# Strassen's algorithm for the last product of a fused three-block kernel, with squares made in the key stage and other buffers for the third-slot sums

## The chip, the core and the metric

The kernel runs on one core of a Trainium2 chip. The core has five engines with an instruction queue each: PE (TensorE, the matrix engine; PEld is its weight load), DVE (VectorE), ACT (ScalarE), POOL (GpSimd) and SP (SyncE, which here only starts DMAs). Matmuls write to PSUM, eight banks of 512 f32 columns on 128 partitions; all other tiles lie in SBUF. The metric is the device time of one execution in microseconds (us), as the median of several runs.

## What is computed

Three blocks follow one another, over 8 batches of 576 tokens (4608 tokens).

```python
# 1. attention by a feature map, 8 heads of 64, phi(x) has 256 features
proj = x @ w_phi; proj -= max|proj|; phi = [exp(proj), exp(-proj)]
kv = phi(k).T @ v; z = sum(phi(k)); attn = (phi(q) @ kv) / (phi(q) @ z)
# 2. four experts of causal softmax attention, head 64, top-2 gates
y_e = softmax(mask((x wq_e)(x wk_e).T / 8)) (x wv_e) wo_e;  x2 = sum_e gate_e * y_e
# 3. token shift and a gated square-ReLU block, 512 -> 1024 -> 512
xk = mu_k * x2 + (1 - mu_k) * x2_prev;  xr likewise with mu_r
k = max(xk @ w_k, 0);  v = (k * k) @ w_v;  r = sigmoid(xr @ w_r);  out = r * v
```

All products are of f32 accuracy: each operand is split into a rounded part (hi, type f32r) and the rest (lo), and three matmuls hi·hi, hi·lo and lo·hi are summed. The last product, (k * k) @ w_v, is 4608 x 1024 x 512. The inputs `w_k`, `w_v` and `w_r` come as 64-bit numbers and are decoded on the chip.

## The kernel before

Five streams of work are written out by Python generators and woven by `weave` (lines 54 to 74), which always takes the next step of the stream that is furthest behind in a virtual time of its own; the costs that steps return and the rates in lines 820 and 826 set that. A scheduler of the language then puts each engine's instructions in an order by these priorities and its own timeline. What a reader finds in the profile is that final order.

- `favors` (lines 250 to 394 and 640 to 663): block 1, batch by batch. Tiles `raw`, `hi`, `lo`, `pj`, `pm`, `ph`, `kv`, `num`, `xt`; the result goes to `XT`. When it is through, its memory is released and `pW` is opened: the last product's weights are loaded from DRAM tiles `wd` into `wst2` and split into `wvh2` and `wvl2` (page names `wvh`, `wvl`).
- `moe1` (lines 397 to 638): block 2. Tiles `qk`, `vp`, `sc` (scores), `a` (softmax), `at` (its transpose), `yp`, `yf`. Each batch's result `yt` is stored to DRAM as `yd`.
- `compose` and `decodes` (lines 188 to 230): the weights. `compose` multiplies the experts' output weights into the token-shifted `w_r` and `w_k` and stores twelve blocks `wf`; `decodes` decodes the sixteen pieces of `w_v` and stores them as `wd`.
- `gates_keys` (lines 676 to 746): the key stage. Tokens are taken in six chunks of 768, as 384 pairs of an even and an odd token. A chunk has twelve units u of 128 outputs (u 0 to 3 gates, u 4 to 11 keys), and each unit three slots `sl`: the product of slot 0 is common to both tokens, those of slots 1 and 2 are added to it for the even and the odd one. One product is six matmuls of 128x384 in a PSUM bank `rk` or `kv`, with weights `wt` loaded on ACT's queue, five buffers deep. ACT evacuates slot 0 into `z` (line 696), DVE adds slots 1 and 2 to it (line 698), and the sum is stored to DRAM tile `kd` on SP's queue (line 699). All `z` lie in one set of four buffers, tag `e`.
- `moe2` (lines 750 to 813): the last product, chunk by chunk and parity by parity. `kt_` loads two units of keys (`kx`), ACT takes ReLU and square in place (lines 777 and 778), DVE makes hi and lo in `XT` (lines 99 and 100), and PE multiplies with `wvh2` and `wvl2`, 96 matmuls of 128x384 into four PSUM banks `vacc` (line 792 through 117). DVE multiplies each bank by the gates `zs`, after ACT's sigmoid (line 764), into `o` (line 802), which is stored to the output.

`weave` in line 820 runs until `moe1` has ended. Then block 2's memory and PSUM banks are released (`phA.close()`), `psB` and `pB` are opened, and line 826 weaves what is left: the end of the key stage (its last chunk may not start earlier) with the last product. The text calls what follows `phA.close()` the last stage.

Of the kernel before, what the change touches and what calls it, by code (L numbers as in the profile page):

```python
# [76 lines left out]
def fused_kernel(ctx: ExitStack, tc: tile.TileContext, qT, kT, vx, wphi, wq, wk, wvg, wo, mu, w64, ident, cmask, tri, out):  # L77
# [9 lines left out]
    wd = [dram.tile([P, 256], F32, name=f'wd{i}') for i in range(NW)]  # L87
# [37 lines left out]
    pQ = ctx.enter_context(tc.tile_pool(name='pQ', bufs=1, side='right'))  # L125
# [514 lines left out]
    def favors():  # L640
# [16 lines left out]
        wv2.extend(pW.tile([P, 8, DM], F32R, name=n) for n in ('wvh2', 'wvl2'))  # L657
        for f in range(8):
            s_ = pW.tile([P, 768], F32, name='wst2', tag='wst2', bufs=2)[:, :512]
            for j in range(2):  # L660
                nc.sync.dma_start(s_[:, j * 256:(j + 1) * 256], wd[24 + 2 * f + j])
            split(wv2[0][:, f], wv2[1][:, f], s_, 'a', nc.gpsimd)
            yield 2000
    wv2 = []
# [11 lines left out]
    def gates_keys():  # L676

        def one(c):
# [3 lines left out]
            def unit(n):  # L682
# [9 lines left out]
                def ev():  # L692
                    z = pR.tile([P, HC], F32, name='z', tag='e', bufs=4)
# [56 lines left out]
    def moe2():  # L750

        def chunk(c, par, os):
            t0 = c * CH
            d = {}
            m = 2 * c + par

            def gate(g):

                def ld():
                    d['z', g] = late['pB'].tile([P, 2, HC], F32, name='zs', tag='zs', bufs=4)  # L760
                    nc.sync.dma_start(d['z', g], kd[c][:, 2 * g:2 * g + 2, par])

                def go():
                    nc.scalar.activation(d['z', g], d['z', g], AF.Sigmoid)
                return [(lambda: 'pB' in late, ld), None, go]

            def kt_(p):

                def ld():
                    if 4 * m + p < 2:  # L770
                        d['s', p] = late['pW'].tile([P, 2 * HC], F32, name='kx', tag='wst2', bufs=2).rearrange('p (u t) -> p u t', u=2)
                    else:
                        d['s', p] = late['pB'].tile([P, 2, HC], F32, name='kx', tag='kx', bufs=6)
# [100 lines left out]
```

## Time and profile before

| | |
|---|---|
| median of 3 runs | 1287.65 us (1284.47 to 1289.37) |
| profiled execution | 1288.14 us, span of its instructions 1286.3 us |
| PE busy | 1241.5 us, 97% of the span |
| DVE busy | 877.7 us, 68% |
| ACT busy | 733.0 us, 57% |
| POOL busy | 412.6 us, 32%, none of it after 1020 us |
| granted clock of TensorE | 0.995 of full speed on the mean |
| DMA | 208.78 MB, 162 GB/s on the mean |

PE has the longest bar and is seldom idle. Busy time of PE is a modelled one: matmuls overlap, and what one costs in a full stream is the distance of two starts, not its duration. So a stretch of the chain of waits in which PE alone stands, divided by the matmuls in it, gives the price of a matmul. Short shares of idle time lie at three places: before 400 us, between 800 and 1045 us, and at the very end, when the last results are stored.

### The profile page before, as it was taken

How to read it: one execution, taken by the hardware profiler on the slowest of the kernel's cores; microseconds unless marked ns; L12 is line 12 of the kernel's file. 1: busy time of each engine (PE TensorE's matmuls, PEld its weight loads, DVE VectorE, ACT ScalarE, POOL GpSimd, SP SyncE). 2: the span in 40 equal slices, each digit the busy share in tenths (PEclk: the TensorE clock that was granted, in tenths of full speed). 3: DMA queues.
4: the chain of work that ended last, by engine and by line, in shares of the span. 5: the costliest groups of instructions: out<-in, count | busy, mean ns of one | idle time of the engine just before them, and what ended most of it. 6: DMA issues, size and time to landing. Idle time of an engine off the chain costs nothing.

```text
span 1286.3 us, 26695 instructions
## 1 busy us (share of the span) xinstructions
PE 1241.5 (97%) x9152; PEld 1201.2 (93%) x9152; DVE 877.7 (68%) x2476; ACT 733.0 (57%) x1836; POOL 412.6 (32%) x570
## 2 busy tenths in 40 slices
PE   8999999999999999999999999879999989999998
PEld 7999989999999999999999999868988989999998
DVE  6766988788977877876788778546677464443441
ACT  5655767678767665665766565645445474333330
POOL 5532566455633323452444343322112100000000
PEclk9999999999999999999999999999999999999999
DMA  6323125322236444455344434766959887988741
GB/s 189 92 75 100 61 81 164 110 73 75 96 99 190 128 116 133 135 167 182 106 138 138 119 103 141 221 192 199 297 179 278 280 287 242 292 287 285 247 146 50
DMA packets 175127, 208.78 MB, mean 162 GB/s; under 512 B 20497, under 2 KB 160145, under 8 KB 174993
## 3 DMA queue, kind: packets, MB, share of 16 engines
q1 hardware_dynamic: 96656, 136.28, 32.6%
q10 hardware_dynamic: 78336, 70.80, 19.3%
q8 instruction: 74, 1.21, 0.4%
q14 instruction: 61, 0.49, 0.1%
HBM read 143.58 MB, written 63.44 MB: 161 GB/s over the span
## 4 chain that ended last, share of the span: by engine, by line
PE 80%; DVE 7%; DMA 5%; ACT 4%; POOL 2%; issue 1%; ACTq 0%; POOLq 0%; DVEq 0%; SPq 0%
PE rk L117 15%; PE vacc L117 14%; PE kv L327 10%; PE num L365 8%; PE qk L117 6%; PE vp L117 4%; PE yp L580 3%; PE at L545 3%; PE pj L275 3%; PE pj L276 2%; PE pj L277 2%; PE fo L117 2%; PE tq L349 2%; PE sc L507 2%; PE sc L508 2%
## 5 line engine op out<-in xcount | busy, mean ns | idle before, releaser
L117 PE MATMUL vacc<-XT,wvh 128*128 128x384 f32 x768 | 198.8, 336 | 3.9 <-DVE o L802 3.5
L100 POOL TENSOR_TENSOR lo<-raw,hi 128x256 fp32r<-128x256 f32 (+1 forms) x160 | 109.7, 688 | 213.7 <-ACT hi L97 203.3
L538 POOL TENSOR_SCALAR a<-a,sv,gw 128x128 f32<-128x128 f32 (+4 forms) x160 | 107.5, 674 | 213.9 <-DVE sv L532 76.1
L117 PEld LDWEIGHTS vacc<-XT,wvh 128*128 128x128 f32 x768 | 139.7, 189 | 4.6 <-DVE o L802 3.9
L365 PE MATMUL num<-kvs,ph 128*128 128x65 f32 (+1 forms) x1280 | 143.7, 262 | 0.0
L365 PEld LDWEIGHTS num<-kvs,ph 128*128 128x128 f32 (+1 forms) x1280 | 137.4, 181 | 4.9 <-issue 1.8
L117 PE MATMUL vacc<-XT,wvl 128*128 128x384 f32 x384 | 127.4, 336 | 0.0
L527 ACT ACTIVATE a<-sc,sv 128x128 f32<-128x128 f32 (+2 forms) x192 | 98.4, 514 | 45.6 <-DVE sv L522 16.4
L285 DVE TENSOR_REDUCE m<-pj 128x4 f32<-128x512 f32 (+1 forms) x160 | 100.6, 631 | 29.9 <-PE pj L277 28.2
L698 DVE TENSOR_TENSOR z<-rk,z 128x384 f32<-128x384 f32 x144 | 79.5, 553 | 59.3 <-PE rk L117 42.4
L287 DVE TENSOR_TENSOR pm<-pj,m 128x512 f32<-128x512 f32 (+1 forms) x160 | 100.0, 630 | 2.6 <-ACT ph L311 0.6
L275 PE MATMUL pj<-wph,hi 128*128 128x256 f32 x288 | 92.4, 321 | 5.4 <-ACT hi L97 4.5
L522 DVE TENSOR_REDUCE sv<-sc 128x1 f32<-128x128 f32 (+2 forms) x192 | 88.3, 469 | 7.4 <-PE sc L508 4.2
L777 ACT ACTIVATE kx<-kx 128x768 f32<-128x768 f32 x48 | 40.1, 841 | 78.8 <-DMA kx<-kd 63.8
L277 PE MATMUL pj<-wph,lo 128*128 128x256 f32 x288 | 83.9, 292 | 0.5 <-POOL lo L100 0.5
L99 DVE CAST XT<-kx 128x768 fp32r<-128x768 f32 x48 | 26.9, 560 | 84.0 <-PE vacc L117 70.0
L276 PE MATMUL pj<-wpl,hi 128*128 128x256 f32 x288 | 83.5, 290 | 0.0
L97 ACT ACTIVATE hi<-raw 128x256 fp32r<-128x256 f32 (+1 forms) x160 | 62.2, 392 | 30.2 <-PE pj L276 11.3
L561 ACT ACTIVATE at1h<-at 128x384 fp32r<-128x384 f32 (+3 forms) x128 | 53.6, 419 | 45.1 <-PE at L545 24.4
L545 PE MATMUL at<-idn,a 128*128 128x128 f32 (+2 forms) x480 | 73.1, 261 | 2.7 <-DVE sv L524 2.4
L117 PEld LDWEIGHTS vacc<-XT,wvl 128*128 128x128 f32 x384 | 72.5, 189 | 0.0
L562 DVE TENSOR_TENSOR at1l<-at,at1h 128x384 fp32r<-128x384 f32 (+3 forms) x128 | 59.5, 466 | 17.8 <-ACT at1h L561 14.1
(487 smaller groups left out, 3438.7 us busy)
## 6 DMA issues: line engine op xcount, KB each, us to landing
wt<-wf ACTq DMA_DIRECT2D x216, 256.0 KB, 3.7
kd<-z SPq DMA_DIRECT2D x144, 192.0 KB, 3.6
kx<-kd SPq DMA_DIRECT2D x48, 384.0 KB, 4.4
yd<-yt SPq DMA_DIRECT2D x16, 864.0 KB, 4.9
zs<-kd SPq DMA_DIRECT2D x24, 384.0 KB, 5.3
out_dram<-o SPq DMA_DIRECT2D x24, 384.0 KB, 4.1
raw<-in_kT_dram SPq DMA_DIRECT2D x64, 128.0 KB, 2.1
raw<-in_qT_dram SPq DMA_DIRECT2D x64, 128.0 KB, 2.2
```

Source lines behind the costliest of these rows:

```text
L100: (el or nc.vector).tensor_sub(lo, src, hi.bitcast(F32))
L117: nc.tensor.matmul(ps, a, m, start=first and i == 0, stop=last and i == n - 1)
L275: nc.tensor.matmul(o, hi[:, c], wph, start=True, stop=False)
L276: nc.tensor.matmul(o, hi[:, c], wpl, start=False, stop=False)
L277: nc.tensor.matmul(o, lo[:, c], wph, start=False, stop=True)
L285: nc.vector.tensor_reduce(m[:, :g], ps, axis=AX.X, op=OP.max, apply_absolute_value=True)
L287: nc.vector.tensor_sub(pm[:, :g * P].rearrange('p (g f) -> p g f', f=P), ps, m[:, :g].unsqueeze(2).to_broadcast([P, g, P]))
L327: nc.tensor.matmul(bank[:, r, :], d['kp'][:, r % 2, c0:c0 + P], d['v'][:, i + (lo_ > 0), r // 2, :], start=new and r == 0, stop=end, skip_ ...
L365: nc.tensor.matmul(ps[lo_:hi_, i, j, :], d['qp'][:, hf, c0 + lo_:c0 + hi_], kvs[hp, b][:, r * 65:(r + 1) * 65], start=hf == 0, stop=hf == 1)
L527: nc.scalar.activation(a[:m, k0:k1_], o, AF.Exp, bias=nm[:m, 0:1], scale=1.0, accum_out=sm[:m, n:n + 1])
L538: eng(asc).tensor_scalar(a[:m, :nk], a[:m, :nk], rc[:m], WT[b][:m, i, e:e + 1], op0=OP.mult, op1=OP.mult)
L545: nc.tensor.transpose(ps[:kw, jj * m:jj * m + m], d['a'][:m, jj * P:jj * P + kw], idn[:m, :m])
```

## The change

The last product is cut into 2 x 2 blocks: the keys by the two halves of the 1024 units and by the parity of the token, the weights by halves of both their dimensions. Winograd's form of Strassen's algorithm then takes seven block products where eight stood. One product j is 24 matmuls of 128x384 into two PSUM banks (dp 0 and 1), so a chunk has 168 matmuls in place of 192. The seven products add up in three pairs of banks, x, y and w: j = 0 starts x, and j = 2, 3 and 4 add to it; j = 1 is y; j = 5 and 6 are w. Between them a bank is read out (`post`), by ACT after j = 0, 2 and 3, by DVE after j = 1, 4, 5 and 6. Four sums of key blocks (`sums`: T1 to T4) are made by DVE on 128x1536 elements; hi comes from ACT and lo from DVE, on 128x1536 too (`parts`). The split parts lie in three slots of `XT`. The weights' four sums are made by POOL where `w_v` is decoded; all seven weight blocks go to a DRAM tile `wc`; four are loaded where `favors` ends, three (`w5`, `w6`, `w2`) at the start of the last stage.

ReLU and square move into the key stage: they stand on ACT between DVE's sum and its store, for u 4 to 11, on 128x384, and what is stored in `kd` is the square. The sums of slot 2 get buffers of their own: two of `wst2` between the end of `favors` and the first load of keys, two of `pB` in the last stage. The keys of chunk 0 are loaded into `wst2` (`k0`) and `XT` ahead of the last stage. Two rates in the weave change (62 for 58 in line 950; in the last stage the key stage starts at 0 with rate 0.85, where it started at 17000 with 1).

```diff
-    wd = [dram.tile([P, 256], F32, name=f'wd{i}') for i in range(NW)]
+    wc = dram.tile([P, 7, 16, 64], F32, name='wc')
...
             hz = (yield from decode(pF, i, dict(tag='pm', bufs=3), 'p'))
-            nc.sync.dma_start(wd[i], hz)
+            a11, a12, a22, a21 = (hz[:, 64 * k:64 * k + 64] for k in range(4))
+            cs = pF.tile([P, 4, 64], F32, name='cs', tag='cs')
+            nc.gpsimd.tensor_add(cs[:, 1], a21, a22)
+            nc.gpsimd.tensor_sub(cs[:, 0], cs[:, 1], a11)
+            nc.gpsimd.tensor_sub(cs[:, 2], a12, cs[:, 0])
+            nc.gpsimd.tensor_sub(cs[:, 3], a11, a21)
+            nc.sync.dma_start(wc[:, 0:3, i - 24], hz[:, :192].rearrange('p (j n) -> p j n', j=3))
+            nc.sync.dma_start(wc[:, 3:7, i - 24], cs)
...
+    def combo(j, k, n, pool, stage, w, tag, bufs):
...
+        nc.sync.dma_start(s_, wc[:, j, q])
+        def go():
+            split(*(x[:, q] for x in WC[j]), s_, 'a', nc.vector if n == 2 else nc.gpsimd)
...
                 def ev():
-                    z = pR.tile([P, HC], F32, name='z', tag='e', bufs=4)
+                    if sl == 2 and 'late' in state:
+                        z = late['pB'].tile([P, HC], F32, name='z', tag='z', bufs=2)
+                    elif sl == 2 and len(WC) == 4 and 'pre' not in state:
+                        z = late['pW'].tile([P, 768], F32, name='z', tag='wst2', bufs=2)[:, :HC]
+                    else:
+                        z = pR.tile([P, HC], F32, name='z', tag='e', bufs=4)
...
                         nc.vector.tensor_add(z, d['p', n], d['m', u])
+                        if u > 3:
+                            nc.scalar.activation(z, z, AF.Relu)
+                            nc.scalar.activation(z, z, AF.Square)
                         nc.sync.dma_start(kd[c][:, u, sl - 1], z)
...
-                    nc.scalar.activation(d['s', p], d['s', p], AF.Relu)
-                    nc.scalar.activation(d['s', p], d['s', p], AF.Square)
...
+        ops = ('b11', 'b21', 'T2', 'T1', 'b22', 'T3', 'T4')
+        wts = (0, 1, 3, 4, 5, 6, 2)
...
+            def sums(j):
...
+                    elif j == 2:
+                        nc.vector.tensor_sub(d['b11'], d['b12'], d['b11'])
+                        d['T1'] = d['b11']
+                        d['T2'] = pB.tile([P, 4, HC], F32, name='kx', tag='kx', bufs=8)
+                        nc.vector.tensor_sub(d['T2'], d['b22'], d['T1'])
+                    elif j == 5:
+                        nc.vector.tensor_sub(d['b12'], d['b22'], d['b12'])
+                    elif j == 6:
+                        nc.vector.tensor_sub(d['b21'], d['b21'], d['T2'])
...
+            def mm(j):
+                    wh, wl = WC[wts[j]]
+                    h, l = slot(7 * c + j)
+                    bank = 'xyxxxww'[j]
+                    for dp in range(2):
...
+                        for f in range(4):
+                            for a, m in ((wh, h), (wh, l), (wl, h)):
+                                nc.tensor.matmul(ps, a[:, f, dp], m[:, f], start=j in (0, 1, 5) and n == 0, stop=n == 11, skip_group_check=True)
...
+                        elif j == 1:
+                            nc.vector.tensor_add(out_(dp, 0)[:, 0], y, d['z', dp])
+                        elif j == 2:
+                            evac('a', d['u2', dp], x)
+                        elif j == 3:
+                            evac('a', d['u4', dp], x)
+                        elif j == 4:
+                            nc.vector.tensor_mul(o, o, g(0, 0))
+                            nc.vector.tensor_mul(out_(dp, 0)[:, 1], x, g(1, 0))
+                        else:
+                            nc.vector.tensor_add(t, w, d['u4' if j == 5 else 'u2', dp])
+                            nc.vector.tensor_mul(out_(dp, 1)[:, 6 - j], t, g(6 - j, 1))
...
-    weave(tc, (fs, 0.0, 1.0, lambda: 0), (rk, 17000.0, 1.0, lambda: 0), (m2, 0.0, 1.0, lambda: 0))
+    weave(tc, (fs, 0.0, 1.0, lambda: 0), (rk, 0.0, 0.85, lambda: 0), (m2, 0.0, 1.0, lambda: 0))
```

SP's queue at the start of the last stage stood like this before, from the store of the last batch of block 2 (`yd`) on; `kx` and `zs` are loads of keys and gates, `kd` a store of a key sum.

```order
L601 DMA yd_113<-yt 256x1x864
L774 DMA kx<-kd_126 128x2x384 x2
L761 DMA zs<-kd_126 128x2x384 x2
L774 DMA kx<-kd_126 128x2x384 x4
L761 DMA zs<-kd_126 128x2x384 x2
L774 DMA kx<-kd_127 128x2x384
```

Now, in the changed kernel, SP's queue from the same store on reads so (`wst` is a weight block, `k_15060` and `k_15062` are the two halves of `k0`, the first keys).

```order
L608 DMA yd_74<-yt 256x1x864
L675 DMA wst_15869<-wc 128x1024
L675 DMA wst_15873<-wc 128x1024
L724 DMA kd_91<-z 128x384 x3
L822 DMA zs<-kd_87 128x4x384
L724 DMA kd_91<-z 128x384
L822 DMA zs<-kd_87 128x4x384
L724 DMA kd_91<-z 128x384
L794 DMA k_15060<-kd_87 128x2x384
L724 DMA kd_91<-z 128x384
L794 DMA k_15062<-kd_87 128x2x384
```

The load of the first keys has moved behind two weight blocks, two gate loads and six stores. On PE, between block 2's last product (`yp`) and the product j = 0 that reads `k0`, the changed order has 90 matmuls of the key stage and the 24 of product j = 1.

DVE's order between two chunks without key work beside it was this before: two halves of one key block at a time (CAST is hi, TENSOR_TENSOR is lo), then the four results.

```order
L99 CAST XT<-kx 128x768
L100 TENSOR_TENSOR XT<-kx,XT 128x768
L99 CAST XT<-kx 128x768
L100 TENSOR_TENSOR XT<-kx,XT 128x768
L802 TENSOR_TENSOR o<-vacc,zs 128x384 x4
```

Now, at the border of the last two chunks, DVE's order is this; lines 904 to 919 are `post`, L848 to L856 make T1, T2, T3 and T4, and L100 makes lo. Ahead of the first row stand a `t<-vacc` (L918, waiting for the second half of product j = 5 of the chunk before the last) and an `XT<-kx` of 128x1536.

```order
L919 TENSOR_TENSOR o<-t,zs 128x384
L100 TENSOR_TENSOR XT<-kx,XT 128x1536
L918 TENSOR_TENSOR t<-vacc,t 128x384
L848 TENSOR_TENSOR kx<-kx 128x1536
L918 TENSOR_TENSOR t<-vacc,t 128x384
L919 TENSOR_TENSOR o<-t,zs 128x384
L851 TENSOR_TENSOR kx<-kx 128x1536
L853 TENSOR_TENSOR kx<-kx 128x1536
L919 TENSOR_TENSOR o<-t,zs 128x384
L856 TENSOR_TENSOR kx<-kx 128x1536
L904 TENSOR_TENSOR o<-vacc,t 128x384
L100 TENSOR_TENSOR XT<-kx,XT 128x1536 x2
```

The last of these rows is lo of T1 and of T2, and PE's order takes T2's product (j = 2) 74 matmuls after the end of that j = 5; all four sums stand ahead of it. Where the key stage was still running, its sums (L698 before, L720 now) stand between such rows in both kernels.

## Rows read from the trace of the kernel before

**Rows 1.** The page's first section: busy us, share and instructions by engine.

```profile
PE 1241.5 (97%) x9152; PEld 1201.2 (93%) x9152; DVE 877.7 (68%) x2476; ACT 733.0 (57%) x1836; POOL 412.6 (32%) x570
```

**Rows 2.** Windows: stretch, length, busy us (instructions) of PE, PEld, DVE, ACT, POOL; clock; DMA.

```profile
400.00:500.00 100.00, 99.92 (x805) 96.35 (x804) 76.04 (x236) 61.75 (x171) 32.74 (x46) 1.00 0.49 147
...
800.00:900.00 100.00, 87.36 (x555) 79.62 (x554) 56.93 (x185) 51.33 (x137) 27.95 (x31) 0.97 0.67 200
...
1100.00:1140.00 40.00, 40.00 (x232) 40.00 (x232) 18.11 (x30) 14.97 (x20) 0.00 (x0) 1.00 0.99 323
...
1260.00:1287.00 27.00, 20.43 (x118) 20.11 (x116) 4.16 (x8) 0.00 (x0) 0.00 (x0) 0.93 0.15 59
```

**Rows 3.** The chain that ended last, its last long piece: start, us, what.

```profile
1215.60 63.28 PE vacc L117 x365
```

**Rows 4.** Groups by form, 1200 to 1287 us: count, busy us, mean ns, idle before.

```profile
L100 DVE TENSOR_TENSOR XT<-kx,XT 128x768 fp32r<-128x768 f32 x12 | 11.5, 958 | 0.4
L802 DVE TENSOR_TENSOR o<-vacc,zs 128x384 f32<-128x384 f32 x20 | 10.4, 556 | 23.0 <-PE vacc L117 23.0
...
L778 ACT ACTIVATE kx<-kx 128x768 f32<-128x768 f32 x7 | 5.9, 848 | 0.2
```

**Rows 5.** Line 100 alone: duration ns min/median/max, first and last start, forms.

```profile
L100 DVE TENSOR_TENSOR wql<-wst,wqh x2: 685/689/693, 11.4 to 12.1; 128x512 fp32r<-128x512 f32 x2
```

**Rows 6.** PE's timeline, 840 to 870 us: start, us, what, idle time ahead.

```profile
847.52 1.33 PE L117 MATMUL rk<-yc__12117,wt 128*128 128x384 f32 x6 [2.08 <-DVE z L698]
...
851.40 1.31 PE L117 MATMUL rk<-yc__11914,wt 128*128 128x384 f32 x6 [0.58 <-ACT z L104]
...
864.71 2.29 PE L117 MATMUL rk<-yc__12047,wt 128*128 128x384 f32 x6 [4.00 <-DMA wt<-wf]
```

**Rows 7.** ACT's timeline, the same stretch.

```profile
845.38 0.84 ACT L777 ACTIVATE kx<-kx 128x768 f32<-128x768 f32 x1 [3.06 <-DMA kx<-kd]
```

**Rows 8.** Windows of 20 us, the same stretch.

```profile
860.00:880.00 20.00, 15.10 (x82) 13.46 (x80) 9.20 (x32) 7.09 (x21) 3.24 (x5) 0.83 0.43 129
```

**Rows 9.** Line 698 alone: what its engine sat idle for, us and times.

```profile
  DMA kd<-z: 12.4, 10
```

**Rows 10.** Line 104 alone: ACT's evacuations of the key stage.

```profile
L104 ACT ACTIVATE z<-rk x72: 470/492/510, 406.5 to 1205.6; 128x384 f32<-128x384 f32 x72
```

**Rows 11.** What PE waited for in the whole span: us, times, longest.

```profile
PE pj L275 <- ACT hi L97: 4.5, 2, 3.8
PE rk L117 <- DVE z L698: 4.1, 5, 2.1
PE sc L507 <- ACT a L527: 4.0, 7, 1.9
...
PE pj L277 <- POOL lo L100: 0.5, 1, 0.5
```

**Rows 12.** DMA issues of the page: count, KB each, us to landing.

```profile
wt<-wf ACTq DMA_DIRECT2D x216, 256.0 KB, 3.7
kd<-z SPq DMA_DIRECT2D x144, 192.0 KB, 3.6
```

**Rows 13.** The chain, 1000 to 1065 us.

```profile
1007.38 0.61 PE yp L580 x6
...
1013.06 3.88 DMA yd<-yt
```

**Rows 14.** Windows of 4 us at the start of the last stage.

```profile
1032.00:1036.00 4.00, 1.75 (x11) 1.43 (x9) 2.66 (x4) 4.00 (x6) 0.00 (x0) 1.00 1.06 369
1036.00:1040.00 4.00, 2.71 (x9) 2.72 (x10) 4.00 (x9) 3.97 (x7) 0.00 (x0) 0.68 0.88 270
1040.00:1044.00 4.00, 4.00 (x22) 4.00 (x21) 3.96 (x7) 3.97 (x6) 0.00 (x0) 0.90 1.04 332
```

**Rows 15.** PE's timeline, 1005 to 1065 us.

```profile
1037.29 0.92 PE L117 MATMUL vacc<-XT,wvh 128*128 128x384 f32 x2 [3.53 <-DVE o L802]
```

**Rows 16.** PE's last row in the timeline.

```profile
1280.09 0.34 PE L117 MATMUL vacc<-XT,wvl 128*128 128x384 f32 x1
```

More of the change, by code (lines that the diff above doesn't have):

```diff
@@ L124, in fused_kernel @@
     XT = pX.tile([P, 16 * S], F32R, name='XT')
-    pQ = ctx.enter_context(tc.tile_pool(name='pQ', bufs=1, side='right'))
+    pQ = phA.enter_context(tc.tile_pool(name='pQ', bufs=1, side='right'))
     wqh, wql, wkh, wkl = (pQ.tile([P, 2, 4, P], F32R, name=n) for n in ('wqh', 'wql', 'wkh', 'wkl'))
@@ L656, in favors @@
         pW = late['pW'] = ctx.enter_context(tc.tile_pool(name='pW', bufs=1))
[L657 to L664, printed above, removed]
+        for j in (0, 1, 3, 4):
+            for k in range(2):
+                combo(j, k, 1, pW, pW, 768, 'wst2', 2)()
+                yield 2000
+    WC = {}
+    def combo(j, k, n, pool, stage, w, tag, bufs):
+        if k == 0:
+            WC[j] = [pool.tile([P, 16, 64], F32R, name=f'wc{x}{j}') for x in 'hl']
+        q = slice(8 * k, 8 * k + 8 * n)
+        s_ = stage.tile([P, w], F32, name='wst2', tag=tag, bufs=bufs)[:, :512 * n].rearrange('p (q n) -> p q n', n=64)
+        nc.sync.dma_start(s_, wc[:, j, q])
+        def go():
+            split(*(x[:, q] for x in WC[j]), s_, 'a', nc.vector if n == 2 else nc.gpsimd)
+            if k + n == 2:
+                WC[j] = [x.rearrange('p (f d h) n -> p f d (h n)', f=4, d=2) for x in WC[j]]
+        return go
     def load_y(c, y, sl, q):
@@ L807, in moe2, with slot @@
-        tasks = []
-        for c in range(NC_):
-            os = {}
-            for par in range(2):
-                g, ks = chunk(c, par, os)
-                tasks += ks + g
-        return skewed(tasks)
+        ops = ('b11', 'b21', 'T2', 'T1', 'b22', 'T3', 'T4')
+        wts = (0, 1, 3, 4, 5, 6, 2)
+        src = {'b11': (0, 0), 'b21': (1, 0), 'b12': (0, 1), 'b22': (1, 1)}
+        def slot(n):
+            return [XT[:, (2 * (n % 3) + x) * 1536:(2 * (n % 3) + x + 1) * 1536].rearrange('p (f t) -> p f t', f=4) for x in range(2)]
@@ new lines, in block, with first @@
+        def block(c, s, par, f0, f1):
+            return kd[c][:, 4 + 4 * s + f0:4 + 4 * s + f1, par]
+        raw = {}
+        def first():
+            while not (done.get(0, 0) == NB and B - 1 in read and len(WC) == 4):
+                yield None
+            state['pre'] = True
+            for i in range(2):
+                raw['b11', i] = late['pW'].tile([P, 2, HC], F32, name='k0', tag='wst2', bufs=2)
+                nc.sync.dma_start(raw['b11', i], block(0, 0, 0, 2 * i, 2 * i + 2))
+            for n, k, x in (('b21', 1, 1), ('b12', 2, 0), ('b22', 2, 1)):
+                raw[n] = slot(k)[x].bitcast(F32)
+                nc.sync.dma_start(raw[n], block(0, *src[n], 0, 4))
+            yield 100000
+            for i in range(2):
+                f = slice(2 * i, 2 * i + 2)
+                split(*(x[:, f] for x in slot(0)), raw['b11', i], 'a')
+                yield 20000
+            for i in range(2):
+                f = slice(2 * i, 2 * i + 2)
+                split(*(x[:, f] for x in slot(1)), raw['b21'][:, f], 'a')
+                yield 20000
+            while 'pB' not in late:
+                yield None
@@ L814, in fused_kernel, with all_ @@
+        def all_():
+            yield from first()
+            yield from skewed([t for c in range(NC_) for t in chunk(c)])
+        return all_()
     clear_pads()
```

129 lines of the change are left out of this document (85 added, 44 removed).

## The prediction

> **What bounds the kernel now.** I read the busy shares first, then the windows, then the end of the chain, and only then the waits. PE has the longest bar, 1241.5 of 1286.3 us [rows 1], and the windows show that this isn't spread evenly [rows 2]: between 400 and 500 us PE is idle for 0.1 us in 100, between 800 and 900 us for 12.6, between 1100 and 1140 us not at all, and the last 27 us hold 6.6 us in which only results are stored. So a matmul taken away in the last stage is time gained, as long as nothing else becomes late there. The chain confirms it: its longest piece is one of last-product matmuls alone, 365 in 63.28 us, or 173.4 ns each [rows 3]. That is the price of a matmul, not the 334 ns that its bar shows, since the next one starts before it ends. Beside PE in the last stage DVE is busy for 18.1 of 40 us, ACT for 15.0, and the DMA engines for 0.99 [rows 2]: the transfers have the least room.
>
> **The change part by part.** All terms are against the profiled execution, 1288.1 us; the median of the runs shown is 0.5 us less.
>
> *Fewer matmuls.* 168 in place of 192 in each of six chunks is 144 fewer, 144 x 173.4 ns = **-25.0 us**. Shape and operand types stay as they were, and twelve in a row on one bank is no new pattern, since the 365 hold runs of 17 on one bank.
>
> *What DVE gets instead.* A 128x1536 lo or sum isn't in the trace. The 128x768 one takes 958 ns [rows 4], the 128x512 one 689 [rows 5]; that is 1.05 ns an element, so 958 + 768 x 1.05 = 1.76 us as an estimate. Bounds: 2 x 958 = 1.92 us if the fixed part counted twice, and 1536 x 1.05 = 1.61 us if it counted not at all. A chunk needs 4 sums and 7 lo's, 11 x 1.76 = 19.4 us, and 14 `post` instructions at the 0.556 us of line 802 [rows 4], 7.8 us: 27.2 us of DVE in the 168 x 0.1734 = 29.1 us that PE takes. While key products lie between, PE has more to do than DVE, but PE's last 350 matmuls have none beside them. There 93% is too full to be smooth. The order shows the place, the border of the last two chunks. From the end of product j = 5 on (its second half) DVE has 8 long rows and 7 short ones up to lo of T2, 8 x 1.76 + 7 x 0.556 = 18.0 us, and PE has 74 matmuls, 12.8 us, before it needs that lo. PE waits for the difference, **+5.2 us**. At the border before it the sums stand early enough. The three borders with key work between cost less: 36 key matmuls add 6.2 us to PE's side and 4 additions 2.2 us to DVE's, which leaves about 1 us; I take +2 for them together. Ends for all borders: 0, and 5 x 5.2 = 26 us.
>
> *Banks read between products.* x is read by ACT after j = 0, 2 and 3. While one half is read, the other half's 12 matmuls run, 2.08 us. An evacuation takes 0.49 us [rows 10], behind at most one 128x1536 hi: 0.848 us for 768 and 0.492 for 384 [rows 4, 10] give 1.56 us for it. 2.05 us fits barely; +1 us, ends 0 and 6.
>
> *The start of the last stage.* Before, the first loads went out when the last `yd` store had landed, 9 us after the last `yp` (1016.9 against 1008.0) [rows 13]. Now two weight blocks, three key stores, two gate loads and more stand between that store and `k0` on SP: 2 x 512 + 2 x 768 + 2 x 384 KB, and six stores of 192 KB [rows 12], 4480 KB. ACT's queue loads 256 KB for every six key matmuls [rows 12]. PE has 114 matmuls until j = 0, 19.8 us; 62 of them are key work that falls after the landing, so ten more weight tiles, 2560 KB. 7.2 MB at the 369 GB/s of the fullest stretch [rows 14] take 19.5 us, so `k0` is there 28.5 us after `yp`, and hi and lo of its first half 1.8 us later [rows 4]: PE waits for 10.5 us, some of it for weights. What before lost in that place goes: a wait of 3.5 us [rows 15], and a granted clock of 0.68 and 0.90 in the eight us after it [rows 14], about 1.7 us. Net **+5 us**; ends 0 (PE is held up less where loads overlap) and +12 (the 270 GB/s of rows 14). The Trainium skill (Perfetto Trace Analysis, Roofline) says that a single active core "is bounded by its 16 DMA engines (~435 GB/s aggregate)"; by that rate the wait would be 3 us shorter. No stretch of this trace moves more than 370 GB/s, so I stay with the row.
>
> *Loads of keys ahead of time.* Before, ACT takes ReLU and square of two early key tiles at 840 to 847 us, and sits 3.06 us in front of one whose load hasn't landed [rows 7]; all behind it on ACT is late, evacuations and the issue of `wt` loads. PE then waits 2.08, 0.58 and 4.00 us [rows 6], and the granted clock is 0.83 on the mean of 20 us, part of it at 1.2 in place of 2.4 GHz [rows 8], 3.4 us more: 10 us in all. That instruction is gone; the first keys are now loaded only when `XT` is free, some 100 us later. But a 10 us hole made by three waits on a crowded queue is rarely emptied by taking one away. I take half, **-5 us**; ends -10 and 0.
>
> *Slot-2 sums in buffers of their own.* DVE sat 12.4 us, 10 times, in front of a `z` whose buffer was still being stored [rows 9], as four buffers serve six sums of a pair of units. PE waited 4.1 us for it [rows 11], 2.1 of it counted above. With squares each buffer is held longer by two ACT instructions, 1 us on top of the 3.6 us of the store [rows 12]. **-1 us**; ends -2 and +4.
>
> *Squares in the key stage.* 96 sums get 2 x 0.49 us of ACT each, 94 us, of which about 70% fall before the last stage: 66 us in 600. ACT's share there rises from 62% [rows 2] to 73%. It evacuates for every stream in turn, so those behind it come later. In the whole span PE waited 8.5 us for ACT's hi and softmax [rows 11]; if queues grow as 1/(1 - share), by 1.4, that is **+4 us**. Ends: 0 (other streams fill PE, as they do at 400 us), and +15.
>
> *No cost.* 64 POOL instructions on 128x64 hide under PE where `w_v` is decoded; PE waited 0.5 us for a POOL lo [rows 11]; ends 0 and +2. In the end the last result needs an addition ahead of its multiplication, **+0.6 us** after PE's last row [rows 4, 16].
>
> Sum: -25.0 + 5.2 + 2 + 1 + 5 - 5 - 1 + 4 + 0.6 = -13.2. 1288.1 - 13.2 - 0.5 is **1274 us**.
>
> **The rivals.** *The matmuls' gain stays whole.* DVE keeps up because lo and sums can be made three slots ahead, the start overlaps, and most of the early hole goes: -25, -8 and small change, **1256 us**. For it: DVE is 45% busy in the last stage [rows 2], and it's in arrears at one border only. Against it: `k0` stands last on a full queue.
>
> *The start is a jam.* `wt`, `k0`, `zs` and the weight blocks come at once; ACT, which takes its instructions in order, stands in front of a weight block that hasn't landed, and key evacuations queue behind it, as behind `kx` in rows 7. With 270 GB/s and a clock that falls after the wait, as in rows 14, that costs 16 us more than before instead of 5: **1285 us**, about no change.
>
> *DVE takes the place of PE.* If what the last border shows holds at all five and at the first (T1 and T2 of chunk 0), 6 x 5.2 = 31 us stand against 25; with the other terms -5 - 1 + 5 + 4 + 1 that is +10: **1298 us**, slower. It decides from 4 us a border on. For it: 27.2 of 29.1 us. Against: key work lies beside three of them, and one without key work has its sums early.
>
> That the change doesn't do what it says I leave aside: the order has 1008 matmuls of the last product.
>
> **How the numbers follow.** Forecast 52%, whole gain 22%, jam 16%, DVE bound 10%. The forecast's own range, by half of its unknown ends, is 1262 to 1286. For 8 in 10 I go to the whole gain below and past the jam above: 1256 to 1292. About 0.5%, 6.4 us, is what a measurement of this kernel can tell. Faster by more than that (under 1281): all of the whole gain and most of the forecast, 0.70. Within it: the jam and the upper end of the forecast, 0.17. Slower: DVE bound and the worst of the jam, 0.13.
>
> **What would show it.** In the profile after, the group of `vacc` has 1008 matmuls, and stretches without waits still give 173 ns. PE's waits by line show one of some 5 us for DVE's lo (line 100) about 120 matmuls from the end; if there is none, 1.76 us or the border is wrong. After the last `yp` there is a hole of about 10 us that ends with the load of `k0` or with lo of it, DMA near 370 GB/s in it. The waits for a `kx` load at 840 us are gone, and PE's idle time between 800 and 900 us falls from 12.6 us to about 8. ACT is busy for 70% or more between 600 and 900 us, and waits for ACT grow to some 12 us. The prediction is wrong as a whole if PE's idle time in the last stage, the tail aside, is over 25 us (DVE or DMA has become the bound), or under 6.

## The result: 1274.8 us, and where the time went

The kernel after takes 1274.81 us in the median (1272.08 to 1278.84), beside 1287.75 for before on the same chip. The ratio is 0.9903, 95% interval 0.9887 to 0.9918. The profiled execution took 1274.73 us, 13.4 less than before's.

The page's first section answers to [rows 1]; two groups by line show the new product and DVE's new size (busy us, mean ns, idle time before).

```profile
PE 1226.7 (96%) x9008; PEld 1183.0 (93%) x9008; DVE 938.4 (74%) x2488; ACT 813.8 (64%) x2003; POOL 429.8 (34%) x634
...
L880 PE MATMUL vacc<-XT,wch 128*128 128x384 f32 x672 | 175.5, 339 | 4.9 <-DVE XT L100 4.1
...
L100 DVE TENSOR_TENSOR XT<-kx,XT 128x1536 fp32r<-128x1536 f32 x40 | 70.1, 1754 | 23.4 <-ACT XT L97 23.4
```

144 matmuls are gone, and the 128x1536 lo takes 1.754 us, where 1.76 was estimated.

To see where the gain went I cut both executions at the end of the last `yp`, where the last stage begins. Windows of PE alone: stretch, length, busy us (instructions), granted clock, DMA share, GB/s. First before:

```profile
1008.00:1300.00 292.00, 268.49 (x1536) 0.99 0.68 223
1008.00:1060.00 52.00, 48.06 (x266) 0.97 0.86 284
...
1220.00:1286.30 66.30, 60.43 (x349) 0.98 0.30 101
```

Then after:

```profile
1006.93:1300.00 293.07, 248.50 (x1375) 0.96 0.68 227
1006.93:1060.00 53.07, 43.95 (x213) 0.87 0.95 322
1060.00:1220.00 160.00, 160.00 (x924) 1.00 0.84 277
1220.00:1272.90 52.90, 44.55 (x241) 0.91 0.26 94
```

A matmul of this stage costs 173.4 ns [rows 3]. The moment of the last `yp` plus the remaining matmuls at that price is when PE would end with no loss; call it E. What the span has beyond E was lost in the last stage.

| | E | lost until 1060 us | lost from 1220 us on | lost in all |
|---|---|---|---|---|
| before | 1008.0 + 1536 x 0.1734 = 1274.3 | 52.0 - 266 x 0.1734 = 5.9 | 5.8 | 12.0 |
| after | 1006.9 + 1375 x 0.1734 = 1245.4 | 16.1 | 11.1 | 27.5 |

So E fell by 28.9 us: 25.0 by the fewer matmuls, 3.9 by something ahead of the last stage. The start of the last stage gave back 10.2 us, its end 5.3. Between 1060 and 1220 us PE never waits. (The stretches don't add up to the last column to the tenth, since a window counts every matmul that touches it.)

The end is the border that was forecast. PE's timeline there:

```profile
1245.26 0.69 PE L880 MATMUL vacc<-XT,wch 128*128 128x384 f32 x1 [3.70 <-DVE XT L100]
```

And the last PE piece of the chain (start, us, what):

```profile
1245.26 23.02 PE vacc L880 x118
```

Ahead of this wait DVE is seldom idle, 0.5 us in 17 (all five engines, as in [rows 2]):

```profile
1228.00:1245.00 17.00, 13.55 (x77) 12.90 (x75) 16.52 (x15) 8.79 (x8) 0.00 (x0) 0.95 0.49 163
```

After 3.7 us of waiting the 118 matmuls take 195 ns each in place of 173.4, which is another 2.6 us; the granted clock is 0.50 from 1245 to 1249 us, 0.85 in the next four and 1.00 from then on. The tail behind them is 1.3 us shorter than before's (1272.9 - 1268.3 against 5.9 us).

The start, in SP's queue (when a DMA was issued, what):

```profile
1016.10 0.80 SPq L675 DMA_DIRECT2D wst<-wc  x2
1017.54 3.58 SPq L724 DMA_DIRECT2D kd<-z  x3
1023.89 0.37 SPq L822 DMA_DIRECT2D zs<-kd  x1
...
1027.24 0.37 SPq L822 DMA_DIRECT2D zs<-kd  x1
1029.45 0.32 SPq L724 DMA_DIRECT2D kd<-z  x1
1029.83 0.43 SPq L794 DMA_DIRECT2D k<-kd  x1
```

`k0` goes out 22.9 us after the last `yp`, behind weights, gates and stores of squares: in the last stage, and not ahead of it as the text on the change has it. ACT, DVE and PE at that time (in brackets the idle time ahead and what ended it):

```profile
1032.61 1.28 ACT L835 ACT_TABLE_LOAD   x1 [0.65 <-PE rk L117]
1033.90 2.86 ACT L835 ACTIVATE zs<-zs 128x1536 f32<-128x1536 f32 x2
1036.66 0.51 ACT L722 ACTIVATE z<-z 128x384 f32<-128x384 f32 x1
1037.24 0.84 ACT L97 ACTIVATE XT<-k 128x768 fp32r<-128x768 f32 x1
...
1035.59 1.22 DVE L720 TENSOR_TENSOR z<-rk,z 128x384 f32<-128x384 f32 x2 [6.70 <-DMA kd<-z]
...
1036.21 4.21 PE L117 MATMUL rk<-yc__14573,wt 128*128 128x384 f32 x12 [4.20 <-DVE z L720]
```

PE's longest hole there ends with an addition of the key stage that sat 6.7 us until a store had released its buffer, not with `k0`. That store is the one issued at 1029.45, which landed 6.0 us later. So the gates' table load and sigmoids, which start at 1032.61, came too late to hold it up. What did is seen in the chain of waits (start, us, what):

```profile
1017.46 8.45 DMA wt<-wf
...
1026.04 2.27 PE rk L117 x6
...
1028.34 0.53 ACTq L769
...
1028.91 0.53 ACT z L723
...
1029.45 0.32 SPq L724
```

A weight load took 8.45 us; PE used it and so freed a weight buffer; ACT's queue issued the next load into it, and only then came to the square that the store had to wait for. In the windows of 4 us around the hole the clock costs about as much as the hole:

```profile
1024.00:1028.00 4.00, 3.38 (x12) 2.92 (x13) 1.69 (x2) 0.93 (x2) 0.00 (x0) 0.61 1.07 359
1028.00:1032.00 4.00, 4.00 (x13) 3.63 (x12) 0.56 (x1) 1.57 (x3) 0.00 (x0) 0.53 1.02 355
1032.00:1036.00 4.00, 0.01 (x1) 0.00 (x0) 0.41 (x1) 3.38 (x3) 0.00 (x0) 0.89 1.06 377
1036.00:1040.00 4.00, 3.79 (x12) 3.79 (x13) 3.26 (x5) 3.89 (x8) 0.00 (x0) 0.50 0.64 225
```

At 0.50, which is 1.2 of 2.4 GHz, PE does 12 matmuls in 4 us where 23 would fit.

### The profile page after: what moved, and what is told of

Read it like the earlier page. It is cut to its first block, busy times and chain, and to the rows that moved or that the text cites. A ratio compares the mean times of both kernels' runs of the same rounds, so it can differ in the third digit from the quotient of the medians.

```text
span 1272.9 us, 26630 instructions
## 1 busy us (share of the span) xinstructions
PE 1226.7 (96%) x9008; PEld 1183.0 (93%) x9008; DVE 938.4 (74%) x2488; ACT 813.8 (64%) x2003; POOL 429.8 (34%) x634
## 4 chain that ended last, share of the span: by engine, by line
PE 76%; DVE 8%; DMA 6%; ACT 4%; issue 2%; POOL 2%; ACTq 1%; SPq 0%; POOLq 0%; DVEq 0%
PE rk L117 13%; PE vacc L880 12%; PE kv L334 9%; PE num L372 8%; PE qk L117 7%; PE vp L117 4%; PE yp L587 3%; PE at L552 3%; PE pj L282 3%; PE pj L283 2%; PE fo L117 2%; PE pj L284 2%; PE tq L356 2%; PE sc L514 2%; PE sc L515 2%
## 5 line engine op out<-in xcount | busy, mean ns | idle before, releaser
L880 PE MATMUL vacc<-XT,wch 128*128 128x384 f32 x672 | 175.5, 339 | 4.9 <-DVE XT L100 4.1
L100 POOL TENSOR_TENSOR lo<-raw,hi 128x256 fp32r<-128x256 f32 (+1 forms) x160 | 109.5, 687 | 171.1 <-ACT hi L97 155.6
L880 PEld LDWEIGHTS vacc<-XT,wch 128*128 128x128 f32 x672 | 123.5, 191 | 6.6 <-DVE XT L100 4.7
L720 DVE TENSOR_TENSOR z<-rk,z 128x384 f32<-128x384 f32 x144 | 79.2, 552 | 49.8 <-PE rk L117 34.7
L880 PE MATMUL vacc<-XT,wcl 128*128 128x384 f32 x336 | 112.4, 338 | 0.0
L100 DVE TENSOR_TENSOR XT<-kx,XT 128x1536 fp32r<-128x1536 f32 x40 | 70.1, 1754 | 23.4 <-ACT XT L97 23.4
L97 ACT ACTIVATE hi<-raw 128x256 fp32r<-128x256 f32 (+1 forms) x160 | 62.3, 392 | 31.8 <-PE pj L283 10.2
L97 ACT ACTIVATE XT<-kx 128x1536 fp32r<-128x1536 f32 x40 | 59.2, 1485 | 30.1 <-PE vacc L880 17.8
L569 DVE TENSOR_TENSOR at1l<-at,at1h 128x384 fp32r<-128x384 f32 (+3 forms) x128 | 59.3, 463 | 16.1 <-ACT at1h L568 13.4
L514 PE MATMUL sc<-k,qs 128*128 128x128 f32 (+2 forms) x192 | 65.6, 351 | 5.4 <-ACT a L534 5.0
```

What stands on the lines that cost most here:

```text
L97: nc.scalar.activation(hi, src, AF.Copy)
L100: (el or nc.vector).tensor_sub(lo, src, hi.bitcast(F32))
L880: nc.tensor.matmul(ps, a[:, f, dp], m[:, f], start=j in (0, 1, 5) and n == 0, stop=n == 11, skip_group_check=True)
```

## The experiments

Ratios are to before, timed on the same chip. "Lost" is as in the table above, from one profile each. How far one profile can be trusted is seen from five kernels below (after, a_sums_early, a_no_gates0, a_gates_dep, c_best6): the order of PE, DVE and ACT is the same in them up to the last `yp`, and E is 1245.4, 1242.4, 1241.5, 1243.5 and 1247.5 us. The three with the first keys in XT (a_k0_in_XT, c_best4, c_best5) have one order too, and there E is 1251.0, 1249.1 and 1243.7.

### Sums of the next chunk made earlier

```diff
-fs = [[load(*l), None, None, None, sums(j), parts(j), None, mm(j), post(j)] for j, l in ...
+fs = [[load(*l), None, sums(j), None, None, parts(j), None, mm(j), post(j)] for j, l in ...
```

In this kernel T1 overwrites b11 before b11 is split, so one product gets other numbers; the work is the same.

> The kernel after, with T1 and T2 of chunks 1 to 5 made two products earlier, and nothing else. Theory 1 (DVE is in arrears only at the border of the last two chunks, because T1 and T2 stand there beside eight results): the wait of 3.7 us for lo, 118 matmuls from the end, falls under 1 us, and the granted clock of the last 50 us, 0.91 in the kernel after, returns to 1.0, which was another 2.5 us; 1274.8 - 5 to 6 = about 1269 us, ratio to before 0.986. Rival (27.2 us of DVE in a chunk's 29.1 us is too full wherever the sums stand): the wait turns up at another product, between 2 and 5 us of it remain, and the ratio stays within 0.0015 of 0.990.

1270.63 us, ratio 0.9860 (0.9831 to 0.9888). There is no wait for lo left at the border; the chain ends with one piece of 174.5 ns a matmul:

```profile
1216.43 46.08 PE vacc L880 x264
```

From 1220 us on 4.7 us are lost in place of 11.1. The border's price is DVE's arrears and the clock behind them, as theory 1 has it. The profile's total doesn't show this by itself: the start loses 18.4 us in this execution, 2.3 more than in after, and E is 3.0 us lower.

### Without the gates of chunk 0

```diff
+if c == 0:
+    nc.gpsimd.memset(d[n], 0.5)
+else:
     nc.sync.dma_start(d[n], kd[c][:, 0:4, int(n[1])])
...
-elif n[0] == 'g':
+elif n[0] == 'g' and c:
     nc.scalar.activation(d[n], d[n], AF.Sigmoid)
```

> The kernel after, with the gates of chunk 0 replaced by a constant 0.5: two loads of 768 KB, ACT's table load (1.28 us) and two sigmoids (2.86 us) at the start of the last stage are left out. Theory 1 (the start is held by the transfers and by ACT standing in front of what they bring): the wait of 4.2 us before the last key products of the start falls under 2 us, PE's idle time between 1007 and 1060 us falls from 9.1 to about 5 us and its mean clock there rises from 0.87 to 0.92; ratio about 0.986. Rival (the start is held by a loop of its own: six sums of a pair of units in four buffers, each held by ACT's two squares and a store of some 4 us): idle time there stays above 8 us, ratio 0.990.

1263.51 us, ratio 0.9797 (0.9771 to 0.9824). The start:

```profile
1003.09:1060.00 56.91, 50.60 (x268) 0.94 0.94 317
```

It loses 56.9 - 268 x 0.1734 = 10.4 us in place of 16.1, and the wait for `z` is 2.6 us, where theory 1 had under 2. Theory 1 in the main, but not through `k0`: that goes out 20.9 us after the last `yp`, only 2 us earlier. Loads and ACT work were left out together, so this run doesn't say which of them counted; by the chain above it wasn't ACT's work that made after's longest hole. The end loses 5.3 us: in the new order the border has no wait, so half of this gain isn't the gates' own.

### Without ReLU and square

```diff
-if u > 3:
-    nc.scalar.activation(z, z, AF.Relu)
-    nc.scalar.activation(z, z, AF.Square)
```

> The kernel after, without ReLU and square (192 ACT instructions of 0.5 us fewer in the key stage, other numbers in the output). Theory 1 (before the last stage other streams fill PE while sums wait for ACT; only the start of the last stage feels the squares): the number of matmuls started by 1007 us stays within 10 of 7635; the start gains about 4 us, as each sum's buffer comes free 1 us earlier; ratio 0.987. Rival (ACT's share of 63 to 74% delays all streams, the +4 us of the forecast): PE is at least 20 matmuls (3.5 us) further at 1007 us, and the ratio is 0.984 or lower. Third: squares cost nothing anywhere, ratio 0.990.

1273.67 us, ratio 0.9877 (0.9849 to 0.9906); an interval that overlaps after's and holds both theory 1's 0.987 and the third's 0.990; 7619 matmuls by 1007 us, 16 fewer than after. So PE is no further without squares ahead of the last stage, and the gain of 4 us at the start did not come. There the hole only changed its name (ACT first, then PE):

```profile
1028.66 9.55 ACTq L766 DMA_DIRECT2D wt<-wf  x5
1038.30 1.28 ACT L832 ACT_TABLE_LOAD   x1 [9.23 <-DMA kd<-z]
...
1043.24 1.01 PE L877 MATMUL vacc<-XT,wch 128*128 128x384 f32 x2 [9.23 <-ACT XT L97]
```

ACT executes nothing for 9.2 us, while its queue issues five weight loads that have to wait for earlier transfers. Behind them stand the gates' table load and sigmoids, and behind those hi of `k0`: the first half of `k0` landed at 1038.9, and its hi started at 1042.36. PE waits 9.2 us for that hi. The DMA engines move 350 to 373 GB/s from 1024 to 1040 us. The start loses 18.2 us without any square: the transfers hold most of it, the gates ahead of hi 3.4 us, and buffers only decide which instruction waits.

### The first keys in XT

```diff
-    raw['b11', i] = late['pW'].tile([P, 2, HC], F32, name='k0', tag='wst2', bufs=2)
+    raw['b11', i] = slot(1)[0].bitcast(F32)[:, 2 * i:2 * i + 2]
...
-elif sl == 2 and len(WC) == 4 and 'pre' not in state:
+elif sl == 2 and len(WC) == 4:
```

(The split of b21 moves behind T1.)

> The kernel after, with the raw first keys of chunk 0 loaded into the second slot of XT in place of wst2, so that the third-slot sums keep wst2 until the last stage opens (in the kernel after they go back to the four shared buffers for that stretch); b21 is split behind T1. Theory 1 (at the start PE waits for an addition that waits for a buffer still being stored): the 4.2 us wait for DVE's z at 1032 us goes, and with it part of the low clock; PE idle between 1007 and 1060 us 9.1 to about 5 us, ratio 0.986. Rival (the transfers as such are the bound of the start): the wait changes its name to wt or XT, idle time stays within 2 us of 9.1, ratio 0.990. As key loads of chunk 1 also move ahead of stores on SP's queue, it may be worse than that: 0.993.

1268.07 us, ratio 0.9839 (0.9810 to 0.9869). The first keys are loaded and split while block 2 still runs:

```profile
1010.46:1060.00 49.54, 43.33 (x233) 0.93 0.91 315
```

The start loses 9.1 us, 7 less. The wait for `z` is 1.0 us, but one of 4.1 us for ACT's `t` has come at 1036 to 1044, with DMA at 372 to 384 GB/s. PE's idle time there falls from 9.1 to 6.2 us, where theory 1 had 5 and the rival 7 or more. Theory 1 for the place of the loss and the ratio; that a wait with full transfers took the old one's place is what the rival said of the cause.

### The gates' loads held back

```diff
+if c == 0:
+    nc.vector.tensor_copy(d[n][:, 0, 0:1], d['T2'][:, 0, 0:1])
 nc.sync.dma_start(d[n], kd[c][:, 0:4, int(n[1])])
```

> The kernel after, in which the loads of the gates of chunk 0 can't start before T2 is made (DVE first copies one column of T2 into each gate tile); nothing is left out. Theory 1 (the gates' 1.5 MB and ACT's 4.1 us of table load and sigmoid are what the start can't carry ahead of the first keys): k0 is issued some 6 us earlier than in the kernel after, the loss of the last stage (its time, less 173.4 ns for each matmul in it) falls from 27.5 to about 17 us, and the ratio to before comes near the 0.980 of the run without these gates. Rival (1.5 MB and two sigmoids must be done anyway, and only move to the next product): the hole turns up at 1045 to 1060 us, the loss stays over 23 us, ratio 0.987 or more.

1267.43 us, ratio 0.9855 (0.9832 to 0.9878), 22.3 us lost: between the theories. Theory 1's way is ruled out: `k0` goes out 24.0 us after the last `yp`, not 6 us earlier than after's 22.9 but 1 us later, as the stores of squares still stand ahead of it on SP. The start loses 16.1 us as before this edit; a hole stands at 1046 us, where the rival had it (ACT, then PE):

```profile
1046.21 0.49 ACT L104 ACTIVATE t<-vacc 128x384 f32<-128x384 f32 x1 [4.43 <-DMA kx<-kd]
...
1046.76 0.61 PE L882 MATMUL vacc<-XT,wch 128*128 128x384 f32 x2 [2.60 <-ACT t L104]
```

The gain is at the end, 5.4 us lost in place of 11.1, as the order there has changed again. Up to `k0` this kernel and the one without gates issue the same loads, but the first weight block was used 7.5 us after its issue here and 4.4 there. So two profiles of a full queue can differ by 3 us in the same place.

### Before without the early key tiles

```diff
-if 4 * m + p < 2:
-    d['s', p] = late['pW'].tile(... tag='wst2', bufs=2) ...
...
-len(wv2) == 2 and (4 * m + p < 2 or 'pB' in late), ld)
+len(wv2) == 2 and 'pB' in late, ld)
```

> The kernel before, without the two early key tiles: the first kx loads wait for the last stage. Theory 1 (the early kx loads make the hole at 840 to 900 us, 10 us in all): PE's idle time between 800 and 900 us falls from 12.6 us to 6 or less, the time until the last yp with the remaining matmuls at 173.4 ns falls by 4 to 8 us; the last stage loses some of it, since its first keys come later. Rival (that stretch is short of work for PE in any case): idle time between 800 and 900 us stays over 10 us and the time is that of before or up to 5 us more.

1292.27 us, ratio 1.0050 (1.0033 to 1.0067): slower. PE's idle time between 800 and 900 us is 10.0 us, not 6, and E is 1276.2. The rival. What the early tiles had saved is seen at the start, which now waits for the first hi:

```profile
1030.13 1.94 PE L117 MATMUL vacc<-XT,wvh 128*128 128x384 f32 x5 [6.38 <-DVE XT L99]
```

### Before with the squares in the key stage

```diff
-nc.scalar.activation(d['s', p], d['s', p], AF.Relu)
-nc.scalar.activation(d['s', p], d['s', p], AF.Square)
...
+if u > 3:
+    nc.scalar.activation(z, z, AF.Relu)
+    nc.scalar.activation(z, z, AF.Square)
```

> The kernel before, with ReLU and square moved into the key stage and nothing else. By the forecast's term (+4 us: ACT's share between 500 and 700 us rises by some ten points and the other streams' evacuations come later) the ratio is 1.003. Rival (other streams fill PE, as the run without squares suggests): the time until the last yp is unchanged within 2 us, and the ratio is 1.000 or, as the last stage has less ACT work, 0.998.

1288.14 us, ratio 1.0007 (0.9991 to 1.0023): the rival's 1.000; the forecast's 1.003 lies outside, and so does 0.998. E is 1276.8, 2.4 us above before's, which is within its scatter. Where before's ACT is busy for 65.65 of 100 us it is now for 75.41, and PE for 98.73, where it had 99.79:

```profile
500.00:600.00 100.00, 98.73 (x792) 94.60 (x792) 77.94 (x233) 75.41 (x198) 41.79 (x59) 1.00 0.49 149
```

### Before with buffers of their own for third-slot sums

```diff
-z = pR.tile([P, HC], F32, name='z', tag='e', bufs=4)
+if sl == 2 and 'late' in state:
+    z = late['pB'].tile([P, HC], F32, name='z', tag='z', bufs=2)
+elif sl == 2 and len(wv2) == 2 and 'pre' not in state:
+    z = late['pW'].tile([P, 768], F32, name='z', tag='wst2', bufs=2)[:, :HC]
+else:
+    z = pR.tile([P, HC], F32, name='z', tag='e', bufs=4)
```

> The kernel before, with third-slot sums in buffers of their own (two of wst2 from the end of favors on, two of pB in the last stage) and, since wst2 is taken, without the two early key tiles: the run without early key tiles plus the buffers. Theory 1 (the buffers are worth about 1 us): PE's waits for DVE's z, 4.1 us before, fall to 2 or less, and the ratio is 0.001 below that of the run without early key tiles. Rival: the four shared buffers were no limit, same ratio within 0.001; or the sums take wst2 from the weights and it is 0.001 above.

1295.40 us, ratio 1.0074 (1.0047 to 1.0101); its interval overlaps that of the run without early tiles, so no gain of the buffers is seen. The profile is of a long execution, 1304.73 us. PE's waits for `z` do fall, to 1.1 us after 800 us, and its idle time between 800 and 900 us to 6.9, as in the kernel after. The time doesn't follow; the first matmuls of the last product wait longer than in the run without early tiles:

```profile
1039.20 1.94 PE L117 MATMUL vacc<-XT,wvh 128*128 128x384 f32 x5 [9.69 <-DVE XT L99]
```

### The start cleared, and then the border

```diff
+if c == 0:
+    nc.gpsimd.tensor_copy(d[n][:, 0, 0:1], d['u2', 0][:, 0:1])
 nc.sync.dma_start(d[n], kd[c][:, 0:4, int(n[1])])
...
+if c == 1:
+    nc.gpsimd.tensor_copy(d[n][:, 0, 0:1], late['u2'][:, 0:1])
 nc.sync.dma_start(d[n], block(c, *src[n], 0, 4))
```

The first copy holds back the gates of chunk 0, the second the keys of chunk 1. c_best4 has this and the first keys in XT.

> The kernel after, with three edits at the start of the last stage: the raw first keys of chunk 0 in XT (as in a_k0_in_XT), and the loads of chunk 0's gates and of chunk 1's keys not before the third product has been evacuated (GpSimd first copies one column of u2 into each tile). Theory 1 (the transfers and ACT's queue at the start are the whole loss there; either edit alone took 5 to 8 us off it): the loss of the last stage falls from 27.5 us to about 10 to 12, of which the tail alone is some 5.5; ratio 0.979. Rival (what is deferred only moves the hole to the next product, or the low clock stays): loss 15 us or more, ratio 0.984 as a_k0_in_XT.

1268.50 us, ratio 0.9856 (0.9824 to 0.9888). The start loses only 51.4 - 271 x 0.1734 = 4.4 us, which is theory 1's part of it, but 17.6 are lost in all and the time is no better than a_k0_in_XT's 1268.07: in time and ratio the rival is right. This order waits for DVE's lo, once at the start (0.9 us) and twice later (us in total, times, longest).

```profile
PE vacc L883 <- DVE XT L100: 4.7, 3, 2.7
```

c_best5 adds the early sums, with `d['T1'] = pB.tile(... tag='kx', bufs=8)` in place of `d['T1'] = d['b11']`, so that b11 stays whole until it is split.

> The same with T1 and T2 of chunks 1 to 5 made two products earlier, T1 in a buffer of its own (output unchanged). Theory 1 (the wait at the last border comes from T1 and T2 standing beside eight results): no wait over 1 us for lo in the last 60 us whatever lies beside it; if the kernel of the run above has that wait, 4 to 6 us faster than it, else the same within 2 us. Rival: the sums crowd another border, 2 to 4 us slower than the run above.

1264.91 us (1258.17 to 1267.89), ratio 0.9811 (0.9779 to 0.9843): 3.6 us less than c_best4, whose interval overlaps this one; after's interval doesn't. In the profile, which is of the shortest execution, 12.7 us are lost, and no wait for lo is left in the last 60 us. It beats both kernels, before by 1.9% and after by 0.9%. The start:

```profile
1003.18:1060.00 56.82, 53.11 (x292) 0.97 0.96 327
```

It loses 56.8 - 292 x 0.1734 = 6.2 us. DMA is as full as in the kernel after (0.96, 327 GB/s), but with what PE needs next.

c_best6 is c_best5 with the first keys in `wst2` again.

> The kernel after, with the deferred loads and the early sums, but with the first keys in wst2 as in the kernel after. Theory 1 (k0 stands behind the stores of squares on SP's queue and is too late in any case): the loss of the last stage stays 5 us or more above the run with the keys in XT; ratio 0.983. Rival (gates and chunk 1's keys were the jam, k0's place doesn't matter): the same as the run with the keys in XT within 2 us.

1270.91 us, ratio 0.9871 (0.9841 to 0.9901), 25.8 us lost, 14.0 of them at the start, 7.8 more than in c_best5; another 6.4 are lost between 1060 and 1220 us. `k0` goes out 23.6 us after the last `yp`. The place of `k0` decides the start; holding gates and chunk 1's keys back is not enough.

### The old rate

```diff
-(rk, 2.6, 62.0 * 1000.0, lambda: -1000)
+(rk, 2.6, 58.0 * 1000.0, lambda: -1000)
```

> The kernel after with the key stage's old rate, 58 in place of 62, until block 2 ends. Theory 1 (the 4 to 8 us that the kernel after gains before the last yp come from key products that the higher rate puts into PE's gaps): 15 to 20 more matmuls remain after the last yp, and the time until then plus the rest at 173.4 ns is 3 us or more above the kernel after's 1241.5 to 1245.4 us. Rival (the third-slot buffers and the early loads that are gone make that gain): unchanged within 2 us.

1296.05 us, ratio 1.0054 (1.0034 to 1.0074): slower than before, with all the rest of the change in it. 1404 matmuls remain after the last `yp`, 29 more than in after, and E is 1255.8 us, 8 to 14 above the five kernels of one order with the rate of 62, and 5 to 12 above the other three. Theory 1, with a larger size. PE's timeline shows where, ahead of the last stage and at its end:

```profile
995.87 0.69 PE L514 MATMUL sc<-k,qs 128*128 128x384 f32 x1 [5.42 <-ACT a L534]
...
1250.32 1.01 PE L880 MATMUL vacc<-XT,wch 128*128 128x384 f32 x2 [4.13 <-ACT XT L97]
...
1261.96 0.44 PE L880 MATMUL vacc<-XT,wch 128*128 128x384 f32 x1 [3.62 <-ACT XT L97]
```

Its windows from 1220 us on:

```profile
1220.00:1294.30 74.30, 56.08 (x296) 0.91 0.40 137
```

23.0 us are lost here in place of 11.1; the start loses 15.2, like after's. I read it so: key products that the rate leaves for later are missing where block 2 leaves PE without work, and the order built from this rate has worse borders. That both follow from the rate is shown, the way from one to the other isn't.

## Why the prediction came out right, step by step

The total was forecast as -13.2 us and came as -13.4, inside the forecast's own case. That the total fits so closely is luck: the start came 5.2 us dearer, and against that the other borders and the banks came 3 us cheaper and the part ahead of the last stage 1.9 us better, the last by a rate that the forecast gave no price.

*Fewer matmuls, -25.0.* Held: 1008 matmuls, 173 ns where nothing waits (160 us for 924).

*The last border, +5.2.* Held in place and cause: 3.7 us of waiting 118 matmuls from the end, 2.6 us of low clock behind it (which was not counted), a tail 1.3 us shorter where +0.6 stood. The other borders (+2) and the banks (+1) cost nothing beyond the 0.7 us that PE waits for ACT's `t` in chunk 0: PE is busy for 160.00 of 160 us from 1060 to 1220 us, at a clock of 1.00. A margin of 7% on DVE was enough wherever the sums stood early.

*The start, +5 net.* Undersized: +10.2, inside its end of +12. The step that failed is the clock, which the sum took off for before (1.7 us) and put at nothing for after. Of the 16.1 us lost until 1060 us 9.1 are waiting, near the 10.5 of the forecast, and 7.0 are low clock; in before it was 3.9 and 1.9. The path was wrong too: the waiting was taken from the landing of `k0`, but PE waits 3.8 us for weight loads, 4.2 for `z`, 0.7 for `t` and 0.4 for a lo of 128x1536, and not once for `k0`. The gates' table load and sigmoids, 4.1 us on ACT, weren't named; in this kernel they don't end in a wait of PE, in the run without squares they do.

That transfers are the bound held, at 355 to 377 GB/s from 1024 to 1036 us. But the forecast says that no stretch of before moves more than 370 GB/s, and 397 are moved from 1060 to 1064 us; at that rate its wait would have been 1.4 us shorter. The rate of some 435 GB/s for one active core (the Trainium skill, Perfetto Trace Analysis, Roofline) was reached in none of these traces' windows of 4 us; the fullest moves 404, in a_sums_early from 1208 to 1212 us.

*Early loads -5, buffers -1, squares +4, together -2.* The sum was seen as -3.9 (E, with a scatter of 6 to 7 us between equal programs), but not from these causes. Taking the early loads away alone makes before 6 us slower; the buffers bring no time; the squares cost 0.9 us, with an interval from -1.2 to 3.0, and the 50 us more that ACT is busy there until 1006 us (676.8 for 626.7) are hidden by the other streams. The hole between 800 and 900 us did shrink, 12.6 to 6.9 us, where about 8 was named; but in the run with buffers on before it shrank as much and E rose to 1281.7: less idle time there is not less time.

*What was to be seen.* The waits for a `kx` load at 840 us are gone, and PE's idle time in the last stage, 9.1 us until 1060 and 3.7 at the border, lies between the 6 and 25 that were set. One hole of 10 us that ends with `k0` isn't there. ACT stays under the 70% named for 600 to 900 us (63, 68 and 69.9%). PE's waits for ACT in the whole span come to 11.9 us where 12 was named, but that is no proof of the queues: the 8.5 us that the forecast multiplied were those for hi and softmax alone, and these are 8.9 now.

*The rates.* The text ahead of the prediction names them, and the prediction gives them no price. That is the step that is missing: 0.9903 against 1.0054 is 1.5%, 19 us, of which the profiles show some 10 before the last `yp` and 12 at the end. In E the rate is worth 10.4 us, more than the 3.9 that were gained there; so at the old rate the rest of the change makes E 6.5 us longer (1255.8 against before's 1274.3 - 25.0), about as much as its scatter. At the old rate the forecast would have been 22 us too low, and the rival with DVE as the bound (1298) nearest, for another reason than its own.

Open: why 62 and not a value near it, as each value gives another order (no other was run, nor before at 62); and the last stage's pair, 0 and 0.85 for 17000 and 1, which was not tried alone.

## What to carry to other kernels

Cut both executions where a stage begins, count the matmuls left, and price them at the pitch of an undisturbed stretch: that tells which stage gave a gain back, where sums of idle time don't, because the clock takes its share without any wait in the trace. A rate in a planner is an edit like any other: price it, since here it was worth more than one and a half times the whole result. And at the opening of a stage ask for each transfer whether PE needs it next. Alone, loading the first keys early was worth 0.6% and moving the sums by two products 0.4%; holding back what is needed later cleared the start (4.4 us lost in place of 9.1) but brought no time beside the early keys, and whether it does beside early keys and early sums wasn't run by itself. All three together are worth 0.9%.

## What the runs showed of the hardware

- With the same order of instructions on PE, DVE and ACT up to the last `yp`, E came out between 1241.5 and 1247.5 us in five executions, and between 1243.7 and 1251.0 in three of another order. An effect under 7 us ahead of that place needs timed rounds, not a profile.
- A hole of 4 us on PE was followed by a granted clock of 0.50 in the next 4 us and 0.75 in the 4 after them (it had been 0.61 and 0.53 from 1024 to 1032 us too, after PE had waited 1.2, 2.0 and 0.6 us); at the end, 3.7 us of waiting by 195 ns a matmul, on the mean, over the remaining 23 us.
- ACT's table load took 1.28 us and the sigmoid of 128x1536 1.43; the 4.1 us of one load and two sigmoids hold a queue in which evacuations and weight loads stand too. In the run without squares hi of the first keys stood behind them and started 3.4 us after its load had landed.
- A store of 192 KB landed 6.0 us after its issue and a weight load of 256 KB after 8.45 us at the start of the last stage, where the whole trace of before has 3.6 and 3.7 us in the median [rows 12].
